# Centring part of the first row tile on ScalarE with the sign turned, all gate products of two tiles ahead of the up products, and later turns of the next tiles

## The chip, the cores and the metric

One core of one Trainium2 chip. The metric is the device time of a whole run in microseconds (us); lower is better. The time before was 921.76 us (median of 4 runs, 921.58 to 922.13).

Engines in the profile: PE is TensorE's matmuls, PEld its weight loads, DVE VectorE, ACT ScalarE, POOL GpSimd, SP SyncE. SBUF is the on-chip memory that the engines read from, PSUM the one that TensorE writes its results to, in banks. To "turn" a tile is to transpose its chunks and copy them to SBUF. "L235" is a line of the kernel. In the changed kernel the same statements have other line numbers: the transpose is L235 before and L244 after, the product L293 and L302, the copy of turned chunks L237 and L246.

## The reference, cut to what matters

```python
x  = A_x                                  # 2048 x 640, bf16
xn = layernorm(x)
s  = attention(xn @ wq, k_cache, v_cache, last 512 keys) @ wo   # 32 heads of 192
h  = sigmoid(xn @ w_gate) * (xn @ w_up)   # w_gate, w_up: 640 x 1536
g  = silu(h @ w_down)
out = x + s * g
```

The kernel computes g first, in four blocks of 512 rows, then the attention. The change touches only the first block's first 512 columns of h: the first 15 us of some 920.

## The kernel before

The first block goes by row tiles of 128 rows, t = 0 to 3. Each tile is centred (mean subtracted), its five 128x128 chunks are transposed on TensorE into PSUM, ScalarE copies the turned chunks to SBUF, and TensorE multiplies them with gate and up weights: five products of 128x512 for gate and five for up. The factor 1/std is not applied to x but later, to the products, so that the products needn't wait for it.

```python
def centred(t, parts=((0, 3 * P), (3 * P, D))):
    xc = xpool.tile([P, D], BF16, name="xn")
    for d0, d1 in parts:
        nc.vector.tensor_scalar(xc[:, d0:d1], xt[t][:, d0:d1], ln[t][:, 0:1], None,
                                op0=ALU.subtract)
    xn_t[t] = xc

def turn_pe(t, c0=0, c1=NCD, k=3):              # NCD = 5 chunks; k: PSUM bank pair
    # pT is in bank[k][:, t % 2, ...], one of the two banks of pair k (line cut)
    for c in range(c0, c1):
        nc.tensor.transpose(pT[:, c, :], xn_t[t][:, c * P:(c + 1) * P], ident[:])
    for d0, d1 in ((c0, c1),) if c1 - c0 < NCD else ((0, 3), (3, NCD)):
        nc.scalar.activation(xcT[:, d0:d1, t * P:(t + 1) * P], pT[:, d0:d1, :], AF.Copy)

def tile_half(t, fg, k, half, c0=0, c1=NCD):    # half 0: gate products, 1: up products
    ...
def tile_gated(t, fg, k):                       # sigmoid on ScalarE, product on VectorE
    ...
# start of the program (... = cuts)
centred(0, ((0, P), (P, 3 * P), (3 * P, D)))
...
turn_pe(0, 0, 1); turn_pe(0, 1, 3, 2); tile_half(0, 0, 0, 0, 0, 1)
turn_pe(0, 3, NCD, 1); tile_half(0, 0, 0, 0, 1)
turn_pe(1, 0, 3); turn_pe(1, 3, NCD, 2)
tile_half(0, 0, 0, 1, 0, 3)                     # up products of tile 0: need w_up
tile_half(1, 0, 1, 0); tile_half(0, 0, 0, 1, 3)
...
tile_gated(0, 0, 0)
for t in range(1, TQ):
    if t > 1:
        tile_half(t, 0, t % 3, 0)
    tile_half(t, 0, t % 3, 1, 0, 1)             # one up product
    if t + 1 < TQ:
        turn_pe(t + 1)                          # turn of the next tile
    tile_half(t, 0, t % 3, 1, 1)                # four up products
    tile_gated(t, 0, t % 3)
```

The softmax here doesn't subtract the row's maximum and nothing guards it: scores larger than these inputs give would overflow.

## Time and profile before

| | before |
|---|---|
| time, median (range) | 921.76 us (921.58 to 922.13) |
| span of the profiled run | 919.2 us |
| TensorE busy | 914.1 us, 99% |
| first product starts | 5.21 us |
| first up product of tile 1 | 9.29 us |
| first gate product of tile 3 | 13.13 us |

The last three rows are landmarks, read from the timeline of TensorE. X is the third product of this one, 8.86 + 2 x 0.216:

```profile
8.86 0.81 PE L293 MATMUL bank<-wu_sb,xnT 128*128 128x512 bf16 x3
```

I use the landmarks throughout. **F** is the first product, **X** the first up product of tile 1, **G** the first gate product of tile 3. The stretch F to X holds the mixed start of tiles 0 and 1. X to G holds the turns of tiles 2 and 3: 15 products and 10 transposes, 15 x 0.216 + 10 x 0.056 = 3.80 us if TensorE never waits. A timeline line gives the start, the length and a count; a product inside a merged line is found by adding 0.216 us for each product before it. Some matmul records are missing from each trace, so a count can be one short.

### The profile page before, as it was taken

To read this page: it belongs to the slowest core of one execution; us is meant where nothing else is said; L and a number is where in the kernel's file an instruction comes from. 1 tells how busy PE (TensorE), PEld (TensorE's weight loads), DVE (VectorE), ACT (ScalarE), POOL (GpSimd) and SP (SyncE) were. 2 spreads that over 40 slices of the span, in tenths; PEclk is the share of its full clock that TensorE was granted. 3 is DMA by queue.
4 is the path that set the end of the run, shared out by engine and by line. 5 is a ranking of instruction groups with operands and counts; after the bars stand their busy time and mean duration, and the time that the engine had idled before them with its cause. 6 is when DMAs were issued, how large, how long until landed. Compare 5 with 4: busy or idle time off the path is not lost.

```text
span 919.2 us, 24974 instructions
## 1 busy us (share of the span) xinstructions
PE 914.1 (99%) x11333; PEld 622.8 (68%) x11333; DVE 492.5 (54%) x989; ACT 302.3 (33%) x332; POOL 134.6 (15%) x159
## 2 busy tenths in 40 slices
PE   9999999999999999999999999999999999999998
PEld 4445455465868686867676777777776767686875
DVE  6462522444646464646555555545564646464667
ACT  4222222255141424242333333242424151515150
POOL 1000100001002000200020011001100111174733
PEclk9999999999999999999999999999999999999999
DMA  9820330115434334342425162515251615253435
GB/s 320 164 44 1 89 87 1 43 62 88 78 63 111 81 64 77 94 98 45 95 85 107 36 104 79 113 31 109 66 108 46 113 61 95 62 120 104 88 84 135
DMA packets 172106, 79.35 MB, mean 86 GB/s; under 512 B 149952, under 2 KB 167568, under 8 KB 172000
## 3 DMA queue, kind: packets, MB, share of 16 engines
q1 hardware_dynamic: 164640, 55.85, 31.1%
q0 software_dynamic: 5808, 20.52, 7.8%
q8 instruction: 88, 1.44, 0.7%
q10 hardware_dynamic: 1552, 1.39, 0.5%
q14 instruction: 18, 0.15, 0.1%
HBM read 39.45 MB, written 2.62 MB: 46 GB/s over the span
## 4 chain that ended last, share of the span: by engine, by line
PE 99%; DMA 1%; DVE 0%; SPq 0%; DVEq 0%; issue 0%
PE bank L517 22%; PE bank L446 21%; PE bank L468 19%; PE bank L428 18%; PE bank L251 8%; PE bank L263 6%; PE bank L293 3%; PE bank L394 1%; DMA wu_sb<-in_B_w_up_dram 1%; PE bank L552 0%; DVE o_sb L498 0%; DVE gate L503 0%; SPq L162 0%; PE bank L235 0%; SPq L167 0%; DVEq L654 0%
## 5 line engine op out<-in xcount | busy, mean ns | idle before, releaser
L432 ACT ACTIVATE E<-bank 128x1024 bf16<-128x1024 f32 x256 | 255.3, 1022 | 456.5 <-PE bank L428 456.4
L446 PE MATMUL bank<-xnT,wq_sb 64*128 64x512 bf16 x1800 | 226.4, 376 | 0.0
L517 PE MATMUL bank<-wo_sb,oT 64*128 64x320 bf16 x2688 | 205.2, 296 | 0.0
L428 PE MATMUL bank<-qT,kT 64*128 64x512 bf16 x1536 | 200.7, 376 | 0.0
L468 PE MATMUL bank<-vbuf,E 64*128 64x193 bf16 x4096 | 195.3, 243 | 0.0
L468 PEld LDWEIGHTS <-E 64*128 64x128 bf16 x4096 | 178.8, 94 | 10.2 <-issue 0.3
L517 PEld LDWEIGHTS <-oT 64*128 64x128 bf16 (+1 forms) x2892 | 163.2, 94 | 30.7 <-issue 0.3
L453 DVE CAST qT<-bank 128x1024 bf16<-128x1024 f32 x90 | 110.2, 1224 | 128.5 <-PE bank L446 128.5
L446 PEld LDWEIGHTS <-wq_sb 64*128 64x128 bf16 x1800 | 106.1, 100 | 87.0 <-issue 0.4
L428 PEld LDWEIGHTS <-kT 64*128 64x128 bf16 x1536 | 88.1, 94 | 73.5
L481 DVE TENSOR_TENSOR o_st<-bank,rden 128x768 bf16<-128x768 f32 x128 | 122.6, 957 | 4.4
L532 DVE TENSOR_TENSOR acc<-bank,acc 128x640 f32<-128x640 f32 x96 | 79.0, 823 | 20.2 <-PE bank L517 20.2
L118 POOL DMA_DIRECT2D vbuf<-in_A_v_cache_dram x28 | 21.1, 753 | 311.0 <-PE bank L468 308.1
L451 DVE COPY seen<-bank 128x2 f32<-128x2 f32 x90 | 14.3, 159 | 79.1 <-PE bank L446 79.1
L480 DVE RECIPROCAL rden<-bank 128x4 f32<-128x4 f32 x128 | 23.4, 182 | 60.6 <-PE bank L468 59.6
L263 PE MATMUL bank<-wd_sb,hT 128*128 128x512 bf16 (+1 forms) x384 | 52.8, 299 | 0.0
L263 PEld LDWEIGHTS <-hT 128*128 128x128 bf16 x384 | 29.7, 98 | 23.1
L251 PE MATMUL bank<-xnT,wg_sb 128*128 128x512 bf16 x180 | 44.7, 379 | 0.0
L251 PE MATMUL bank<-xnT,wu_sb 128*128 128x512 bf16 x180 | 44.7, 379 | 0.0
L257 DVE TENSOR_TENSOR hT<-bank,sig 128x512 bf16<-128x512 f32 x36 | 24.8, 690 | 37.1 <-ACT sig L254 37.1
L254 ACT ACTIVATE sig<-bank 128x512 bf16<-128x512 f32 x36 | 21.5, 597 | 55.8 <-PE bank L251 52.7
L97 POOL DMA_DIRECT2D wq_sb<-in_A_wq_dram x7 | 6.3, 900 | 210.7 <-PE bank L446 210.7
(51 smaller groups left out, 406.1 us busy)
## 6 DMA issues: line engine op xcount, KB each, us to landing
wo_sb<-in_A_wo_dram SPq DMA_DIRECT2D x7, 960.0 KB, 5.6
wq_sb<-in_A_wq_dram POOLq DMA_DIRECT2D x7, 960.0 KB, 6.1
k_st<-in_A_k_cache_dram POOLq DMA_DIRECT2D x14, 384.0 KB, 5.6
vbuf<-in_A_v_cache_dram POOLq DMA_DIRECT2D x28, 192.0 KB, 3.5
row<-in_A_x_dram POOLq DMA_DIRECT2D x16, 160.0 KB, 2.7
oT<-o_st SPq DMA_TRANSPOSE x128, 3.4
x_sb<-in_A_x_dram SPq DMA_DIRECT2D x3, 640.0 KB, 9.4
wd_sb<-in_B_w_down_dram SPq DMA_DIRECT2D x1, 1920.0 KB, 14.4
```

What stands on the lines that cost most here:

```text
L251: nc.tensor.matmul(bank[k][:, half, 0:r1 - r0], lhsT=w[:, c, f * P:(f + 1) * P], rhs=xnT[:, b, c, r0:r1], start=(c == 0), stop=(c == NCD - 1))
L257: nc.vector.tensor_tensor(hT[b][:, f, r0:r1], bank[k][:, 1, 0:r1 - r0], sig[:, 0:r1 - r0], ALU.mult)
L263: nc.tensor.matmul(wide(k)[:, d0:d1], lhsT=hT[b][:, f, q * P:(q + 1) * P], rhs=wd_sb[:, f, d0:d1], start=(f == 0), stop=(f == NF - 1))
L293: nc.tensor.matmul(bank[k][:, half, :], lhsT=xcT[:, c, t * P:(t + 1) * P], rhs=w[:, c, fg * FT:(fg + 1) * FT], start=(c == 0), stop=(c == ...
L428: nc.tensor.matmul(bank[k][:, i, :], lhsT=kT[r, pr, j, c * P:(c + 1) * P], rhs=q[r, pr * DJ + j, :], start=(j == 0), stop=(j == DJ - 1))
L432: nc.scalar.activation(E[u, pr][:, c, :, :], bank[k][:], AF.Exp, scale=scale_qk)
L446: nc.tensor.matmul(bank[k][:, half, :], lhsT=wq[r, c, col:col + DJ * (P - 1) + 1:DJ], rhs=xnT[r, b, c, :], start=(c == 0 and not second), ...
L453: nc.vector.tensor_copy(qT[u][:, 2 * m:2 * m + 2, :], bank[k][:])
L468: nc.tensor.matmul(o4[:, q, 0:DH + 1], lhsT=e[r, c, h % 2, q * P:(q + 1) * P], rhs=vbuf[r, h, c, 0:DH + 1], start=(turn == 0 and qq == 0 a ...
L481: nc.vector.tensor_tensor(o_st[u][:, :, h * DH:(h + 1) * DH], o4[:, :, 0:DH], rden[:].to_broadcast([P, TQ, DH]), ALU.mult)
L517: nc.tensor.matmul(res[:, half, :], lhsT=oT[u][r, cc, q * P:(q + 1) * P], rhs=wo[r, cc, half * HD:(half + 1) * HD], start=(turn == 0 and c ...
L532: nc.vector.tensor_tensor(cols(acc[:, t, :]), res, cols(acc[:, t, :]), ALU.add)
```

## The change

The intent, as far as the diff shows it: take 256-wide pieces of the centring off VectorE at the very start, so that tile 1 is centred sooner; fill the wait for the up weights with the gate products of tile 1; and put the turns of tile 1 among the gate products of tile 0. ScalarE computes bias + scale * x, so with the mean as bias it gives mean - x. The sign is turned everywhere, and the factor is negated on GpSimd. The up products before each turn become three instead of one.

```diff
 def stats_root(t):
+    if t < TQ:
+        minus[t] = bwork.tile([P, 1], F32, name="minus")
+        nc.gpsimd.tensor_scalar(minus[t][:], rstd[:], -1.0, None, op0=ALU.mult)
...
-def centred(t, parts=((0, 3 * P), (3 * P, D))):
+def centred(t, parts=((0, 3 * P), (3 * P, D)), on_act=0):
     ...
+    for i, (d0, d1) in enumerate(parts):
+        if i < len(parts) - on_act:
+            nc.vector.tensor_scalar(xc[:, d0:d1], xt[t][:, d0:d1], ln[t][:, 0:1], -1.0,
+                                    op0=ALU.subtract, op1=ALU.mult)
+        else:
+            nc.scalar.activation(xc[:, d0:d1], xt[t][:, d0:d1], AF.Identity,
+                                 bias=ln[t][:, 0:1], scale=-1.0)
...
 def tile_gated(t, fg, k, between=None):
-    rstd = ln[t][1]
+    rstd = minus[t]
...
-centred(0, ((0, P), (P, 3 * P), (3 * P, D)))
+centred(0, ((0, P), (P, 3 * P), (3 * P, D)), 2)
...
-tile_half(0, 0, 0, 0, 1)
+tile_half(0, 0, 0, 0, 1, 3)
 turn_pe(1, 0, 3)
+tile_half(0, 0, 0, 0, 3)
 turn_pe(1, 3, NCD, 2)
-tile_half(0, 0, 0, 1, 0, 3)
 tile_half(1, 0, 1, 0)
-tile_half(0, 0, 0, 1, 3)
+tile_half(0, 0, 0, 1)
...
-tile_gated(0, 0, 0)
 for t in range(1, TQ):
     ...
-    tile_half(t, 0, t % 3, 1, 0, 1)
+    tile_half(t, 0, t % 3, 1, 0, 3)
     if t + 1 < TQ:
         turn_pe(t + 1)
-    tile_half(t, 0, t % 3, 1, 1)
+    tile_half(t, 0, t % 3, 1, 3)
+    if t == 1:
+        tile_gated(0, 0, 0)
     tile_gated(t, 0, t % 3)
```

More of the change, by code (lines that the diff above doesn't have):

```diff
@@ L222 @@
         xn_t = {}
-        def centred(t, parts=((0, 3 * P), (3 * P, D))):
+        minus = {}
+        def centred(t, parts=((0, 3 * P), (3 * P, D)), on_act=0):
             xc = xpool.tile([P, D], BF16, name="xn")
-            for d0, d1 in parts:
-                nc.vector.tensor_scalar(xc[:, d0:d1], xt[t][:, d0:d1], ln[t][:, 0:1], None,
-                                        op0=ALU.subtract)
+            for i, (d0, d1) in enumerate(parts):
[5 more added lines that the diff above has]
+                                         bias=ln[t][:, 0:1], scale=-1.0)
             xn_t[t] = xc
```

## The prediction

> **What bounds the kernel now.** I read the page first: busy shares, then the chain that ended last, then the idle time in the groups.
>
> ```profile
> PE 914.1 (99%) x11333; PEld 622.8 (68%) x11333; DVE 492.5 (54%) x989; ACT 302.3 (33%) x332; POOL 134.6 (15%) x159
> ...
> PE 99%; DMA 1%; DVE 0%; SPq 0%; DVEq 0%; issue 0%
> ...
> L446 PE MATMUL bank<-xnT,wq_sb 64*128 64x512 bf16 x1800 | 226.4, 376 | 0.0
> L517 PE MATMUL bank<-wo_sb,oT 64*128 64x320 bf16 x2688 | 205.2, 296 | 0.0
> ```
>
> TensorE works 914.1 of 919.2 us, the chain is TensorE for 99%, and the big matmul groups have no idle time before them. So the change, which keeps every product and every transpose and only changes their order and what feeds them, can win or lose only bubbles of the TensorE stream, all in the first 13 us. The waits of the weight loads (PEld) up to 16 us show how much there is:
>
> ```profile
> PEld L293 <- ACT xnT L237: 1.4, 4, 0.5
> PEld L194 <- DVE warm L169: 1.1, 1, 1.1
> PEld L235 <- DVE xn L227: 0.3, 1, 0.3
> PEld L293 <- issue: 0.2, 1, 0.2
> ```
>
> Then the timeline of TensorE from 4 us, to place them (columns: start us, length us, engine, line, operation, names, shapes; L235 is a transpose, L293 a product):
>
> ```profile
> 4.54 0.48 PE L235 MATMUL bank<-ident,xn 128*128 128x128 bf16 x3
> 5.21 0.38 PE L293 MATMUL bank<-wg_sb,xnT 128*128 128x512 bf16 x1 [0.19 <-DMA wg_sb<-in_B_w_gate_dram]
> 5.43 0.27 PE L235 MATMUL bank<-ident,xn 128*128 128x128 bf16 x2
> 5.54 1.24 PE L293 MATMUL bank<-wg_sb,xnT 128*128 128x512 bf16 x4
> 6.62 0.44 PE L235 MATMUL bank<-ident,xn 128*128 128x128 bf16 x5
> 7.14 0.81 PE L293 MATMUL bank<-wu_sb,xnT 128*128 128x512 bf16 x3
> 7.78 1.24 PE L293 MATMUL bank<-wg_sb,xnT 128*128 128x512 bf16 x5
> ```
>
> A 512-wide product follows another every 0.216 us (later five take 1.08), a transpose every 0.056 us; the printed lengths contain overlapping drain. From the first transpose (4.54) to the gate product of row tile 3 (13.13, below) there are 20 transposes and 30 products: 20 x 0.056 + 30 x 0.216 = 7.60 us of work in 8.59 us. So the bubbles there sum to about 1.0 us: 0.14 and 0.35 before the first product, 0.21 within the first tile's gate products (four products and the one step to the next transpose take 6.62 - 5.54 = 1.08, of which 0.87 is work), 0.24 before the first up product (7.14; its weights landed at 7.10), and 0.03 at the turn of tile 2. This 1.0 us, 0.11% of the time, is all that the change could win. From 7.14 on the chain names nothing but TensorE.
>
> **What the Trainium skill says.** "TensorE: Matmul & The Clock Gate", section "Back-to-back issue gap", gives N/2.4 + 2.5 ns for a warm product, 216 ns at 512: the trace agrees (0.216). The same page, section "Step-by-step: what each phase is for", says that weight loads are pulled ahead but matmuls stay in program order, so a product that waits holds up all behind it; the trace shows no product out of program order. "ScalarE: Activation LUTs", section "What ACT_TABLE_LOAD costs", gives 186 ns + 0.833 N ns with immediates and about 93 ns more for each pointer operand, and back-to-back overlap of about 93 ns. In the trace, the 512-wide sigmoid with a pointer scale takes 687 ns and that without 597, a difference of 90, and the two copies of one turn overlap by about 0.10. The same page, section "Table sets: the hidden batching unit", says that copy and identity are in every set; the trace has Copy after Sigmoid with a single table load, and Identity isn't shown yet.
>
> **Part 1, centring on ScalarE.** Of three VectorE pieces of tile 0 (254, 281 and 282 ns, beginning 4.23, last end 4.88) the two 256-wide ones go to ScalarE. Each: 186 + 93 + 213 = 492 ns, an estimate from that page's figures (the trace's 256-wide copy from PSUM with immediates is 383). The means are ready at 4.20, so ScalarE runs 4.25 to 4.75 and 4.65 to 5.15. VectorE had ended these chunks at 4.68 and 4.88: 0.07 and 0.27 later, not earlier. ScalarE is in order and the copy of the first turned chunk (4.81 before) comes behind both in the program: about 5.05 to 5.33, so the first product goes from 5.21 to 5.38. In exchange VectorE starts on tile 1 0.39 us earlier: its first centred piece ends at 5.88 in place of 6.27. Turning the sign with a second immediate operation I count as free.
>
> **Part 2, new order of the first two tiles.** I ran the list forward with the latencies of the trace: VectorE to weight load 0.05, last transpose's end to copy 0.04, copy to weight load 0.05. Gate products of tile 0: c0 5.38; transposes 3 and 4 5.60; c1, c2 5.71; three transposes of tile 1 6.14 (their data is ready at 5.93, so the earlier VectorE is used); c3 6.35, c4 6.57; the other transposes 6.79. Free at 6.90. Now the gate products of tile 1 need the copy of the three chunks: last transposed at 6.47, copied 6.51 to 6.99, first product 7.05: a bubble of 0.15 replaces the wait for the up weights. Ten products, then the first up product of tile 1 at 7.05 + 10 x 0.216 = 9.21, where before it was at 9.29. **Gain 0.09 us**, most of it uncertain.
>
> **Part 3, the turns of tiles 2 and 3.** The turn of the next tile now comes after three up products, leaving two between the turn and the next gate product, where there were four. Before, at tile 3:
>
> ```profile
> 11.99 0.44 PE L235 MATMUL bank<-ident,xn 128*128 128x128 bf16 x5
> ...
> 12.27 1.03 PE L293 MATMUL bank<-wu_sb,xnT 128*128 128x512 bf16 x4
> 12.47 0.77 ACT L237 ACTIVATE xnT<-bank 128x384 bf16<-128x384 bf16 x2 [0.87 <-PE bank L235]
> 13.01 17.06 PEld L293 LDWEIGHTS <-xnT 128*128 128x128 bf16 x80 [0.21 <-ACT xnT L237]
> 13.13 1.24 PE L293 MATMUL bank<-wg_sb,xnT 128*128 128x512 bf16 x5
> ```
>
> Read it as a race. ScalarE's copy starts when all five transposes have ended (12.43, not the third); it takes 0.49, and the next weight load is released at 13.01: 1.02 us after the first transpose. TensorE meanwhile has 0.28 of transposes and 4 x 0.216 = 0.86 of products, 1.14 us: the copy is hidden with 0.12 to spare. With two products TensorE has 0.28 + 0.43 = 0.71 us and must wait 1.02 - 0.71 = **0.31 us, at tile 2 and again at tile 3**: 0.62. Saved: the 0.03 at tile 2, which came from a sigmoid ahead of the copy, as the sigmoid of tile 0 now stands behind it. The deferred sigmoid and product of tile 0 hold bank 0 until about 2.6 and 3.3 us after that 9.21; tile 3 wants it 4.4 us after, so no wait from there.
>
> **Part 4, the negated factor on GpSimd.** Four operations on 128x1. The power operations take 548 ns, so the negations take at most about that. The first factors are ready by about 8 us, the first sigmoid now runs after 10.5. Off the path.
>
> **Sum.** -0.09 + 0.62 - 0.03 = +0.5 us. Nothing absorbs a shift afterwards as TensorE streams to the end: 921.93 + 0.5 = 922.4.
>
> **Rivals.** (a) **The intent holds**: earlier VectorE and the gate-first order take away the 0.21 and 0.24 bubbles and the turns cost nothing: -0.4 us, 921.5. For it: both bubbles exist, and the wait for weights does go. Against it: the copy's 0.80 from the last transpose to the product is longer than two products. It would need the copy to start at the third transpose, and then 0.20 would still be left each time: about +0.25 in total. (b) **Table loads**: if Identity needed another set, a load of 1.28 us (the trace's one load) before the centring and one back before the sigmoid; the first is on the path and costs over 1.2 us, the second stands mostly beside products: 923.5 to 924.5. The page speaks against it. (c) **ScalarE is the bound at the start**: if its SBUF-source pieces take 0.6 each, everything in part 2 is 0.1 to 0.2 later and the gain is gone: 922.5 to 922.7. (d) **No visible change**: 0.5 us is as wide as the spread of the three runs (921.6 to 922.13), so the medians may hardly differ.
>
> **Range and chances.** Half of the 0.5 us is run spread, and (a) to (c) lie from 921.5 to 924. I give 921.6 to 923.0 eight in ten. Over 2% is 18 us; no rival comes near: same 0.98.
>
> **What would show it.** Right: in the timeline of the changed kernel, two new idle times of about 0.3 us of the weight loads behind the copies L237 near 10.5 to 11 and 13 to 13.5 us; pieces of about 0.49 us on ScalarE from 4.25; first product near 5.4; first up product of tile 1 near 9.2; one table load. Wrong: no idle weight load at those turns (rival a), a second table load (b), pieces far from 0.49 (c), or a TensorE bubble after 14 us that the kernel before lacks.

## The result, and the profile after

The changed kernel took **922.54 us** (median of 4 runs, 921.88 to 923.38) against 921.76. The ratio is 1.0008, with a 95% interval from 0.9991 to 1.0026. A ratio here is the mean time of one kernel's runs over that of the other's in the same rounds, so it is not quite the ratio of the medians quoted. The interval includes no change at all: what follows rests on the traces more than on the times.

The timeline of TensorE in the changed kernel (start us, length us, engine, line, operation, names, shapes, count, idle before):

```profile
5.74 0.38 PE L302 MATMUL bank<-wg_sb,xnT 128*128 128x512 bf16 x1 [0.69 <-DMA wg_sb<-in_B_w_gate_dram]
...
8.50 1.89 PE L302 MATMUL bank<-wu_sb,xnT 128*128 128x512 bf16 x8
10.23 0.44 PE L244 MATMUL bank<-ident,xn 128*128 128x128 bf16 x5
10.72 0.38 PE L302 MATMUL bank<-wu_sb,xnT 128*128 128x512 bf16 x1
11.25 1.25 PE L302 MATMUL bank<-wg_sb,xnT 128*128 128x512 bf16 x5 [0.15 <-ACT xnT L246]
...
12.99 0.44 PE L244 MATMUL bank<-ident,xn 128*128 128x128 bf16 x5
13.27 0.59 PE L302 MATMUL bank<-wu_sb,xnT 128*128 128x512 bf16 x2
14.01 1.25 PE L302 MATMUL bank<-wg_sb,xnT 128*128 128x512 bf16 x5
```

The reader is to see the starts, not the printed idle times, which the modelled drain of a product shortens. After the turn at 12.99 come two up products, 13.27 and 13.48; the next could start at 13.70, and starts at 14.01. That is 0.31 us of nothing, and the same again before 11.25 (the last up product started at 10.72; 10.94 would have been possible). X is at 8.50 + 5 x 0.216 = 9.58, so X to G is 14.01 - 9.58 = 4.43 us where it was 3.84.

The waits of the weight loads up to 16 us, one line, to hold against the first line of the same view before (columns: total us, times, longest):

```profile
PEld L302 <- ACT xnT L246: 2.0, 5, 0.6
```

The wait for ScalarE's copies went from 1.4 to 2.0 us. What ScalarE did, from its timeline:

```profile
1.65 1.28 ACT L187 ACT_TABLE_LOAD   x1 [1.65 <-DVE wg_sb L172]
...
4.21 0.91 ACT L236 ACTIVATE xn<-x_sb,mv 128x256 bf16<-128x256 bf16 x2 [1.06 <-DVE mv L206]
...
10.71 0.77 ACT L246 ACTIVATE xnT<-bank 128x384 bf16<-128x384 bf16 x2 [2.86 <-PE bank L244]
```

The two centring pieces take 0.91 us together from 4.21, and there is still one table load. The copy at 10.71 stands right behind the end of the fifth transpose; ScalarE had been idle for 2.86 us before it, so it isn't ScalarE's load that makes the product late.

And the negation, from the groups of GpSimd in the first 16 us (count | busy us, mean ns | idle before):

```profile
L216 POOL TENSOR_SCALAR minus<-rstd 128x1 f32<-128x1 f32 x4 | 0.9, 224 | 0.4
```

**Where the span went.** The spans are 919.2 and 920.7 us, 1.5 apart; the profiled runs' times are 921.03 and 922.45. By landmarks: F is 0.53 later (5.74 - 5.21), as the first gate weights landed at 5.70; F to X is 0.24 shorter (3.84 for 4.08); X to G is 0.59 longer; and from G to the end the changed kernel took 906.7 and the kernel before 906.1. 0.53 - 0.24 + 0.59 + 0.6 = 1.5. Only two of these four terms were in the prediction as such. The experiments had to tell which of them belong to the change.

### The profile page after: what moved, and what is told of

Same layout as the page of the kernel before. It is cut to its first block, busy times and chain, and to the rows that moved or that the text cites. A ratio compares the mean times of both kernels' runs of the same rounds, so it can differ in the third digit from the quotient of the medians.

```text
span 920.7 us, 24960 instructions
## 1 busy us (share of the span) xinstructions
PE 913.5 (99%) x11314; PEld 623.1 (68%) x11333; DVE 494.3 (54%) x987; ACT 302.9 (33%) x334; POOL 134.9 (15%) x163
## 3 DMA queue, kind: packets, MB, share of 16 engines
q10 hardware_dynamic: 1552, 1.39, 0.5%
## 4 chain that ended last, share of the span: by engine, by line
PE 98%; DVE 1%; DMA 0%; issue 0%; ACT 0%; DVEq 0%
PE bank L527 22%; PE bank L456 21%; PE bank L478 19%; PE bank L438 18%; PE bank L260 8%; PE bank L272 6%; PE bank L302 3%; PE bank L404 1%; DMA wg_sb<-in_B_w_gate_dram 0%; PE bank L562 0%; DVE gate L513 0%; DVE o_sb L508 0%; ACT xnT L246 0%; PE bank L244 0%; DVEq L664 0%
## 5 line engine op out<-in xcount | busy, mean ns | idle before, releaser
L527 PE MATMUL bank<-wo_sb,oT 64*128 64x320 bf16 x2688 | 205.2, 296 | 0.0
L478 PE MATMUL bank<-vbuf,E 64*128 64x193 bf16 x4096 | 195.3, 243 | 0.3 <-DVE o_sb L508 0.3
L478 PEld LDWEIGHTS <-E 64*128 64x128 bf16 x4096 | 178.8, 94 | 10.7 <-issue 1.1
L527 PEld LDWEIGHTS <-oT 64*128 64x128 bf16 (+1 forms) x2892 | 163.4, 94 | 30.6 <-issue 0.3
L272 PE MATMUL bank<-wd_sb,hT 128*128 128x128 bf16 (+1 forms) x377 | 52.4, 298 | 0.4
```

Source lines behind the costliest of these rows:

```text
L272: nc.tensor.matmul(wide(k)[:, d0:d1], lhsT=hT[b][:, f, q * P:(q + 1) * P], rhs=wd_sb[:, f, d0:d1], start=(f == 0), stop=(f == NF - 1))
L478: nc.tensor.matmul(o4[:, q, 0:DH + 1], lhsT=e[r, c, h % 2, q * P:(q + 1) * P], rhs=vbuf[r, h, c, 0:DH + 1], start=(turn == 0 and qq == 0 a ...
L527: nc.tensor.matmul(res[:, half, :], lhsT=oT[u][r, cc, q * P:(q + 1) * P], rhs=wo[r, cc, half * HD:(half + 1) * HD], start=(turn == 0 and c ...
```

## The experiments

Twelve runs were made, of nine new kernels and of three kernels once more, all with correct results. This is the list of landmarks from all profiles, in us, with the medians of the timed runs beside those of the kernel before in the same rounds:

| run | F | X | G | F to X | X to G | median | before |
|---|---|---|---|---|---|---|---|
| kernel before | 5.21 | 9.29 | 13.13 | 4.08 | 3.84 | 921.76 | |
| e12, before again | 5.39 | 9.73 | 13.57 | 4.34 | 3.84 | 921.47 | 921.81 |
| changed kernel | 5.74 | 9.58 | 14.01 | 3.84 | 4.43 | 922.54 | 921.76 |
| e10, changed again | 5.46 | 9.31 | 13.75 | 3.85 | 4.44 | 922.26 | 921.71 |
| e1, turn after 1 | 5.33 | 9.18 | 12.98 | 3.85 | 3.80 | 921.29 | 921.63 |
| e11, turn after 1 again | 5.34 | 9.78 | 13.58 | 4.44 | 3.80 | 921.45 | 921.71 |
| e2, before, turn after 3 | 6.22 | 10.06 | 14.50 | 3.84 | 4.44 | 922.15 | 921.63 |
| e3, turn after 5 | 5.62 | 9.86 | 15.16 | 4.24 | 5.30 | 922.85 | 921.63 |
| e9, copies of 2 and 3 | 5.39 | 9.25 | 13.47 | 3.86 | 4.22 | 921.70 | 921.71 |
| e5, turn in two calls | 5.44 | 9.29 | 14.61 | 3.85 | 5.32 | 923.16 | 921.53 |
| e4, no ScalarE centring | 5.33 | 9.49 | 13.92 | 4.16 | 4.43 | 922.30 | 921.63 |
| e6, before, ScalarE centring | 5.45 | 9.63 | 13.46 | 4.18 | 3.83 | 922.03 | 921.53 |
| e7, before, order alone | 5.34 | 9.62 | 13.45 | 4.28 | 3.83 | 921.66 | 921.53 |
| e8, first weights in two | 5.43 | 9.45 | 13.24 | 4.02 | 3.79 | 922.15 | 921.53 |

The column X to G is what repeats: it differs by at most 0.01 us between profiles of kernels that have the same turns and the first sigmoid at the same place (ahead of the first copy in the kernel before, e6 and e7, 3.83 to 3.84; behind it in e1, e11 and e8, 3.79 to 3.80). F and F to X move from run to run with the same program (e1 against e11, before against e12).

### Are the later turns the loss? (e1, e2)

```diff
 # e1: the changed kernel with
-            tile_half(t, 0, t % 3, 1, 0, 3)
+            tile_half(t, 0, t % 3, 1, 0, 1)
             if t + 1 < TQ:
                 turn_pe(t + 1)
-            tile_half(t, 0, t % 3, 1, 3)
+            tile_half(t, 0, t % 3, 1, 1)
 # e2: the kernel before with the opposite edit
```

Expected of e1:

> The changed kernel with one thing put back: the turns of tiles 2 and 3 come after one up product again (four products between turn and gate product). Theory (two products are too short to hide the copy): the two idle times of about 0.31 us on TensorE behind the turns of tiles 2 and 3 vanish, from the first up product of tile 1 to the first gate product of tile 3 takes 3.80 us in place of 4.43, and the time falls by 0.6 us against the changed kernel, to 0.1 us of the kernel before. Rival (the loss comes from the centring on ScalarE or from the start's loads): that stretch stays within 0.1 us of 4.43 or the time stays at +0.5 us or more over before.

Expected of e2:

> The kernel before with only the turns of tiles 2 and 3 moved behind three up products. Theory: the stretch from the first up product of tile 1 to the first gate product of tile 3 grows from 3.84 to about 4.43 us (twice 0.31 of idle, less the 0.03 wait behind the sigmoid), and the time grows by 0.6 us. Rival (it takes the change's other parts to lose): the stretch and the time stay within 0.1 us of before.

The timeline of TensorE in e1:

```profile
8.10 1.46 PE L302 MATMUL bank<-wu_sb,xnT 128*128 128x512 bf16 x6
9.40 0.44 PE L244 MATMUL bank<-ident,xn 128*128 128x128 bf16 x5
9.68 1.03 PE L302 MATMUL bank<-wu_sb,xnT 128*128 128x512 bf16 x4
10.54 1.24 PE L302 MATMUL bank<-wg_sb,xnT 128*128 128x512 bf16 x5
...
12.98 1.24 PE L302 MATMUL bank<-wg_sb,xnT 128*128 128x512 bf16 x5
```

Turn at 9.40, four products from 9.68, gate product at 10.54: 9.68 + 4 x 0.216, no gap. X to G is 3.80, the floor. In e2 it is 4.44, as in the changed kernel, with none of the change's other parts: turns at 10.71 and 13.48, and the gate products behind them at 11.74 and 14.50, 1.03 and 1.02 us later. So the later turns alone add 0.6 us to this stretch, in either kernel, and taking them back removes it. The rivals of both runs are out as far as the stretch goes. In time, e1 measured 921.29 against 921.63 and e2 922.15 against 921.63: in the expected directions, both with intervals that include 1 (0.9982 to 1.0007; 0.9992 to 1.0017), so the times alone settle neither.

### Does the idle follow the race of copy against products? (e3, e9)

```diff
 # e3: the changed kernel with the turn after all five
-            tile_half(t, 0, t % 3, 1, 0, 3)
+            tile_half(t, 0, t % 3, 1)
             if t + 1 < TQ:
                 turn_pe(t + 1)
-            tile_half(t, 0, t % 3, 1, 3)
 # e9: the changed kernel with the first copy of two chunks
-            for d0, d1 in ((c0, c1),) if c1 - c0 < NCD else ((0, 3), (3, NCD)):
+            for d0, d1 in ((c0, c1),) if c1 - c0 < NCD else ((0, 2), (2, NCD)):
```

Expected of e3:

> The changed kernel with the turns after all five up products, none left to hide the copy. Theory (race of 1.02 us against 0.28 plus 0.216 for each product): idle of 0.74 us at each of two turns, the stretch from the first up product of tile 1 to the first gate product of tile 3 takes 5.29 us, the time rises by 0.86 us over the changed kernel. Rival (an idle time of fixed length from the semaphores or from PSUM): the idle stays near 0.31 each, and the time that of the changed kernel.

Expected of e9:

> The changed kernel with the copies of the turns of tiles 2 and 3 cut as two and three chunks in place of three and two; the program of TensorE is untouched. Theory (the idle behind a turn is the wait for the first copy): that copy takes 0.38 in place of 0.49 us, so the idle falls from 0.31 to 0.21 at each turn and the stretch from the first up product of tile 1 to the first gate product of tile 3 from 4.43 to 4.22 us; the second copy is still in time for the third product. Rival (the product waits for both copies, or for the transposes alone): the stretch stays at 4.43 or grows.

TensorE in e3, then in e9:

```profile
10.94 0.44 PE L244 MATMUL bank<-ident,xn 128*128 128x128 bf16 x5
11.96 1.25 PE L302 MATMUL bank<-wg_sb,xnT 128*128 128x512 bf16 x5 [0.58 <-ACT xnT L246]
```

```profile
9.89 0.44 PE L244 MATMUL bank<-ident,xn 128*128 128x128 bf16 x5
10.17 0.59 PE L302 MATMUL bank<-wu_sb,xnT 128*128 128x512 bf16 x2
10.81 1.25 PE L302 MATMUL bank<-wg_sb,xnT 128*128 128x512 bf16 x5
```

In e3 the gate product follows the turn by 11.96 - 10.94 = 1.02 us, the length of the race that the prediction read off the kernel before, with only 0.28 us of transposes beside it. X to G is 5.30 for an expected 5.29, and the time is 922.85 against 921.63 (ratio 1.0013, 1.0001 to 1.0026: the interval excludes no change). The expected rise of 0.86 us over the changed kernel isn't to be seen in the times: the medians, from different rounds, are 0.31 apart. In e9 the product follows by 0.92 in place of 1.02, just what a first copy of 0.38 in place of 0.49 us gives, and X to G is 4.22 as expected. Dose and response agree for zero, two and four products behind the turn and for two lengths of the copy. Its time, 921.70 against 921.71, is lower than the changed kernel's 922.26 of the same rounds, though the ranges overlap (921.56 to 922.89 and 921.84 to 922.79).

### What does the first copy wait for? (e5)

```diff
             if t + 1 < TQ:
-                turn_pe(t + 1)
+                turn_pe(t + 1, 0, 3)
+                turn_pe(t + 1, 3, NCD)
```

> The changed kernel with the turns of tiles 2 and 3 still after three up products, but each turned and copied in two calls (three chunks and their copy, then two chunks and their copy), which lets the first copy wait for the third transpose only. Theory (the copy waits for the last transpose that was put into the program ahead of it on the same bank, then 0.80 us to the product): the copy starts 0.11 us earlier, the idle time falls from 0.31 to about 0.20 us at each turn, the stretch from the first up product of tile 1 to the first gate product of tile 3 takes about 4.20 us in place of 4.43. Rival (the wait is for something else, such as the bank's earlier readers): the stretch stays at 4.43.

A miss: X to G is 5.32, not 4.20, and the time is 923.16 against 921.53, the slowest of all. TensorE in e5:

```profile
9.98 0.33 PE L244 MATMUL bank<-ident,xn 128*128 128x128 bf16 x3
10.89 0.27 PE L244 MATMUL bank<-ident,xn 128*128 128x128 bf16 x2 [0.58 <-ACT xnT L246]
```

The first half of the expectation held: the copy started at 10.35 in ScalarE's timeline, 0.37 us after the first transpose, where it had been 0.48 (10.23 to 10.71 in the changed kernel). The second half failed: the other two transposes waited until that copy had ended, 0.74 us after they could have started (9.98 + 3 x 0.056 = 10.15). They write other columns of the same bank that the copy reads. The Trainium skill, "PSUM — Partial Sum Buffer", section "PSUM bank collisions raise a hardware error", says that accesses of two engines to one bank (and the same group of 32 partitions in it) have to be kept apart by semaphores whatever their addresses. The traces agree with a program that waits by bank: a copy waits for the last transpose put ahead of it on its bank, and a later transpose waits for the copy. The other three bank pairs are in use at that point (tile 0's results not yet taken, tile 1's being summed, tile 2's next). But the turn uses only one bank of its own pair, `t % 2`; whether the last two chunks could go to the other one, so that they don't wait, was not tried.

### What are the new start's parts worth? (e4, e6, e7)

```diff
 # e4: the changed kernel, all of tile 0 centred on VectorE
-        centred(0, ((0, P), (P, 3 * P), (3 * P, D)), 2)
+        centred(0, ((0, P), (P, 3 * P), (3 * P, D)))
 # e6: the kernel before with minus and centred() of the changed kernel, order as before
-        centred(0, ((0, P), (P, 3 * P), (3 * P, D)))
+        centred(0, ((0, P), (P, 3 * P), (3 * P, D)), 2)
-            rstd = ln[t][1]
+            rstd = minus[t]
 # e7: the kernel before, order of tiles 0 and 1 alone; turns of tiles 2, 3 after one product
-        tile_half(0, 0, 0, 0, 1)
+        tile_half(0, 0, 0, 0, 1, 3)
         turn_pe(1, 0, 3)
+        tile_half(0, 0, 0, 0, 3)
         turn_pe(1, 3, NCD, 2)
-        tile_half(0, 0, 0, 1, 0, 3)
         tile_half(1, 0, 1, 0)
-        tile_half(0, 0, 0, 1, 3)
+        tile_half(0, 0, 0, 1)
```

Expected of e4:

> The changed kernel with all three pieces of tile 0 centred on VectorE, sign still turned. Theory: the first product is then bound by the arrival of its weights; tile 1's centring ends some 0.4 us later, its transposes wait for it, and from the first product to the first up product of tile 1 takes up to 4.2 us in place of 3.84 when the weights come early, so the time is 0 to 0.2 us above the changed kernel. Rival (ScalarE's queue at the start is what costs the 0.5 us): the time falls by 0.2 us or more.

Expected of e6:

> The kernel before with the centring of two pieces of tile 0 on ScalarE and the turned sign alone. Theory: in the old order the earlier VectorE helps nobody, as the transposes of tile 1 come after all gate products of tile 0; from the first product to the first up product of tile 1 takes 3.84 to 4.08 us as the up weights land late or early against it, from there to the first gate product of tile 3 3.80 to 3.84; the time stays within 0.3 us of before. Rival (the centring on ScalarE gains or costs by itself): one of the stretches leaves these limits, or the time moves by 0.5 us or more.

Expected of e7:

> The kernel before with the gate products of both tiles first and the split turn of tile 1 among those of tile 0, all centring on VectorE, turns of tiles 2 and 3 after one product. Theory: with early weights the transposes of tile 1 wait for VectorE, and the stretch from the first product to the first up product of tile 1 is about 4.15 us, as in the changed kernel without ScalarE centring (4.16), no better than the 4.08 of before; the second stretch is 3.80 to 3.86; the time within 0.3 us of before. Rival (the order alone is the gain): 3.84 us or less in the first stretch with a first product before 5.4 us.

e4 against e1, which have the same F of 5.33: without ScalarE's share the transposes of tile 1 waited for VectorE, started at 6.39 in place of 6.10, and F to X grew from 3.85 to 4.16 us. So with early weights the ScalarE centring was worth 0.31 us in the new order, by one profile of each. One part of the expectation missed: the copy of the first chunk (from 5.00 us), and not the weights, released the first product of e4. Its time, 922.30, is 0.24 below the changed kernel's 922.54, as the rival asked, but from other rounds, and 0.04 above that of e10: not resolved. e6 put the same centring into the old order: X to G as expected at 3.83, F to X 4.18, a little outside of the limits named (3.84 to 4.08), which by the letter is the rival's sign; 922.03 against 921.53, not resolved. e7, the order alone: F to X 4.28 for an expected 4.15, 921.66 against 921.53.

The two misses of 0.1 us have a visible cause: in e6 and e7 (and e3 and e11) the first products ran at a slower pace. In e11 the transpose behind the first product started 0.40 us after it, in e1 0.22. The Trainium skill, "TensorE: Matmul & The Clock Gate", section "What's actually happening", says that the array starts at half its clock and that the moment of the full pace differs between runs of one kernel; by the formula for the slow pace in its section "Back-to-back issue gap", N/1.2 ns, 512 columns would take 427 ns (an estimate). The traces agree, with 0.40. In e7 the slow pace also hid what was to be tested: VectorE had the first three chunks of tile 1 centred at 6.31 us, and TensorE came to their transposes only at 6.53. So e7 doesn't tell whether the order alone gains anything. The pace makes F to X comparable only between profiles that were at full pace by then: before, e12, changed, e1, e2, e4, e5, e8, e9 and e10.

### The kernels once more (e10, e11, e12)

No edits: the changed kernel and e1 side by side in one set of rounds, and a second profile of the kernel before.

> The changed kernel itself once more, beside the version with the turns after one product, to compare them on one chip. Theory: stretch from the first up product of tile 1 to the first gate product of tile 3 again 4.43 us; the first product starts when its weights land, somewhere from 5.3 to 6.2 us, otherwise than in its first profile; the time 0.3 to 0.8 us over the kernel before.

> The changed kernel with the turns after one product, once more in the same rounds. Theory: 0.6 us (0.4 to 0.9) below the changed kernel and within 0.4 us of the kernel before, the stretch 3.80 us. Rival: what the first comparison showed was luck of the loads, and the two agree within 0.2 us.

> The kernel before itself, for a second profile of its start. Theory (the start differs from run to run by the arrival of the first loads and by when TensorE reaches its full pace): the first product lies somewhere from 5.2 to 6.2 us, the stretch from it to the first up product of tile 1 anywhere from 3.84 to 4.3 us, and from there to the first gate product of tile 3 3.80 to 3.84 us as before. Rival (the start of the kernel before is always as in its first profile): 5.21 and 4.08 us again within 0.05.

On one chip the changed kernel took 922.26 us (921.84 to 922.79) and the version with turns after one product 921.45 (920.94 to 921.51): the ranges of five runs each don't overlap, 0.81 us between the medians. The turns account for 0.64 (4.44 - 3.80). But that the two numbers are close is chance: the spans of the two profiles also differ by 0.8, and by landmarks e11 against e10 has -0.12 in F, +0.59 in F to X (the slow pace), -0.64 in X to G and -0.6 from G to the end. e10's first product was not set by its weights, which landed at about 5.2 (issued at 1.17, 4.0 us to landing), but by ScalarE's copy: F was 5.46. That part of its expectation missed.

e12 refutes its rival (5.39 and 4.34 for 5.21 and 4.08; 4.34 is 0.04 above the range expected) and shows what the start of the kernel before hangs on. First the chain of work in the first profile of the kernel before, then in e12, then in e1 (start us, length us, what):

```profile
2.13 4.96 DMA wu_sb<-in_B_w_up_dram
7.10 0.04 issue
7.14 2.53 PE bank L293 x11
```

```profile
2.14 5.40 DMA wu_sb<-in_B_w_up_dram
7.53 0.04 issue
7.58 2.53 PE bank L293 x11
```

```profile
4.19 0.91 ACT xn L236 x2
5.09 0.19 ACT xnT L246
5.28 0.05 issue
5.33 0.39 PE bank L302
```

In both profiles of the kernel before, X is the landing of the up weights plus 2.2 us, and that landing moved from 7.10 to 7.53: X moved from 9.29 to 9.73. In e1 the chain runs through ScalarE's centring and the up weights are not in it. In the changed kernel's own first profile it was the load of the first gate weights.

### An attempt to beat both (e8)

```diff
-        load_f(nc.scalar, wg_sb, wg_r, 0, 4, 0, 3)
+        load_f(nc.scalar, wg_sb, wg_r, 0, 4, 0, 1)
+        load_f(nc.scalar, wg_sb, wg_r, 0, 4, 1, 3)
```

This is e1 with the first load of gate weights cut in two.

> Meant to beat both: the changed kernel with the turns after one product, and the first load of gate weights (three chunks, 384 KB, that landed between 5.0 and 6.2 us in the runs so far) cut in two, chunk 0 first. Theory (the start is set by the arrival of these weights in most runs, and that differs from run to run by over 1 us): chunk 0 lands before 5.0, the first product starts at 5.3 behind the copy on ScalarE, chunks 1 and 2 arrive no later than now; the time is 921.0 to 921.3, some 0.3 to 0.5 us below the kernel before of the same rounds, with less spread. Rival (bandwidth: the loads behind are delayed by as much, or chunk 1 becomes the wait): the first product or the second waits as now and the time is that of the turns after one product alone.

It failed by its rival: chunk 0 landed early, 2.7 us after its issue, and F was 5.43, behind the copy. But chunks 1 and 2 landed only at about 5.9, and the second product started at 5.94 where 5.77 would have followed the transposes. The time was 922.15 against 921.53, with a spread from 921.71 to 925.08, more and not less (ratio 1.0013, 1.0000 to 1.0026). That is more than the turns after one product took; why, was not looked into.

So the best version is e1. Its ten runs in two sets of rounds lie from 920.94 to 921.51, and those of the kernel before from 921.16 to 922.61. Both intervals of the ratio (0.9982 to 1.0007 and 0.9982 to 1.0009) include 1, so that it beats the kernel before is likely but not settled; that it beats the changed kernel by some 0.8 us is seen in the same rounds.

## Why the prediction was right or wrong

The time was right: 922.54 us measured, 922.4 predicted, range 921.6 to 923.0. That the median came so close is in part luck, as the steps show; the difference from the kernel before is itself not resolved by the times.

**What bounds the kernel** was right: TensorE is 99% busy in all profiles and what the change moved lies before 14 us, with one exception told below. But bubbles don't lie in the first 13 us alone: from 860 to 919 us TensorE was busy for 55.45 of 59 us in the kernel before.

**Part 1** was right in its mechanism and sizes. The pieces took 507 and 492 ns for an estimate of 492, from 4.21; the second one ended at 5.12 for 5.15. Turning the sign cost VectorE nothing: three pieces take 0.65 us in e4 as before. VectorE began on tile 1 at 4.36 in e1 and 4.51 in e10, where it was 4.79 before; in the first profile of the changed kernel it waited for the rows of tile 1 until 4.91. The first product behind ScalarE's copy was put at 5.38; where the weights came early it was at 5.33 to 5.46 (e1, e5, e9, e10). The first profile of the changed kernel had 5.74, as its weights landed at 5.70, which the prediction did not reckon with.

**Part 2** had the stretch right, and the gain ill-founded. F to X was put at 9.21 - 5.38 = 3.83 and measured 3.84 and 3.85. But "Gain 0.09 us" set a forecast against the one X of one profile, 9.29, and that X hangs on a load whose landing moved by 0.43 us between two profiles of the same kernel. The new order takes this load off the chain; what that is worth depends on the loads. X lay at 9.29 and 9.73 before and at 9.58 and 9.31 in the changed kernel, so that a pair of profiles shows anything from 0.29 lost to 0.42 gained. And the old order has 3.84 as well when its first product comes late enough that the up weights are there: e2, with F at 6.22. The mechanism stands; the size of the gain is not shown.

**Part 3** was right. Idle of 0.31 us twice was predicted; X to G grew by 0.59 and 0.60 us for the 0.62 less 0.03 predicted. e1 and e2 show that it is the turns, e3 and e9 that it is the race.

**Part 4** was right, with room: the negation takes 224 ns for at most 548.

**The sum** left a term out. "Nothing absorbs a shift afterwards as TensorE streams to the end" looks only for gaps that would close, and the last sentence named "a TensorE bubble after 14 us that the kernel before lacks" as a sign of being wrong. There is one. GpSimd, VectorE and TensorE in the changed kernel, late:

```profile
880.02 1.39 POOL L547 TENSOR_TENSOR acc<-acc,row 128x640 f32<-128x640 f32 x1 [0.75 <-DMA row<-in_A_x_dram]
880.13 1.96 DVE L513 TENSOR_TENSOR gate<-o_sb,acc 128x640 bf16<-128x640 f32 x1
...
882.02 0.81 DVE L508 TENSOR_TENSOR o_sb<-bank,gate 128x640 f32<-128x640 f32 x1
...
882.88 0.84 PE L478 MATMUL bank<-vbuf,E 64*128 64x193 bf16 x16 [0.29 <-DVE o_sb L508]
```

The first VectorE operation (L513) takes 0.82 us when nothing is beside it. Here it took 1.96, with a GpSimd operation on the same kind of tile from 880.02 to 881.41; the next VectorE operation freed a bank 1.1 us late, and TensorE went on at 882.88 where its rhythm (0.65 us after 881.76) would have had it at 882.41. The Trainium skill, "SBUF — State Buffer", section "SBUF: two separate sides", says that VectorE and GpSimd share a port pair, that a VectorE operation with two SBUF inputs and a GpSimd operation that reads SBUF exclude each other, and that the one which starts second fully blocks. The traces agree: the longer one ended 0.68 us after GpSimd's (at 881.41 + 0.68), as in e10 and in the kernel before (0.69 each), where a whole one takes 0.82; and in e2, where the VectorE operation began first (880.62, GpSimd 880.63), it kept its 0.82 us and GpSimd took 2.07 in place of 1.39.

From G to the end the changed kernel took 906.7 us in both its profiles, and the kernel before 906.1 in both of its own (919.7 - 13.57 = 906.1 for e12). The whole difference arises here: from G to the last group of L527 products ahead of this place (L517 before) it is 865.62 us in both profiles of the changed kernel and 865.61 and 865.60 in those of the kernel before; the next stretch, up to the fifth group of L478 products (L468), takes 7.25 and 7.30 against 6.72 in both of the kernel before. So of the 1.5 us between the first two profiles 0.5 to 0.6 is this collision.

Is it of the change's making? The other profiles speak against a simple link. e2 and e4 have the same late turns and show no such stop of TensorE (906.1 and 906.4 from G to the end); e8 has its turns after one product and shows it (906.7). The rest lie between 906.1 (e11) and 906.5. GpSimd's start there is released by the landing of a row of x, so where TensorE stands against the loads can decide who collides; whether the changed kernel makes it more frequent, or two profiles out of two were chance, stays open. The prediction's 0.5 us came out near the measured 0.8 with this term not counted at all, with a start whose gain or loss changes from run to run, and with times that scatter by 0.5 us and more.

**Rivals.** (a), the turns cost nothing, is refuted by X to G; its remark that a copy released by the third transpose would still leave 0.20 each was not testable, as e5 shows, because the bank is held. (b), table loads: one load, refuted. (c), ScalarE slower at 0.6 us a piece: refuted by 507 and 492 ns. (d), no visible change in the times: true of every single comparison of the changed kernel with the kernel before.

## What to carry to other kernels

When work is moved behind other work on a full engine, count what is left in front of the consumer: here two products (0.43 us) could not hide a turn, a copy and a release (1.02 us with the transposes' own 0.28), and four could. A gain measured against one profile of a start that waits for loads is worth no more than the spread of those landings, so take two profiles of the kernel before ahead of such a change. And within a few tenths of a microsecond, compare stretches between landmarks in the trace that depend on no load and begin after TensorE has its full pace: X to G repeated to 0.01 us where the times of one kernel scatter by 0.5 us and more, and F to X did not (3.85 and 4.44 in e1 and e11).

## What the Trainium skill lacked or had wrong

- "PSUM — Partial Sum Buffer", "PSUM bank collisions raise a hardware error": it gives the rule by bank and quadrant, and not what it costs a pipeline. Here a copy of chunks 0 to 2 that waits for transposes 3 and 4 of the same bank starts 0.11 us later (0.48 against 0.37 us after the first transpose), and two transposes that wait for a copy on their bank lost 0.74 us.
- "TensorE: Matmul & The Clock Gate", section "What you observe": the step to full pace is put about 4 us into sustained work, give or take 0.5 (the next section calls it run-variable). The spread was wider here. TensorE started at about 1.05 us in these kernels. In the first profile of the kernel before, the last two of its 256-wide warm-up products started 0.10 us apart (4.16 and 4.26), where they had been 0.21 apart until 4.02; in e11 a 512-wide product at 5.96 us still took 0.42. So the step came from at most 3.2 (4.26 - 1.05) to at least 5.3 us (6.38 - 1.05) after the start, though in e11 with short waits of TensorE on the way.
- "TensorE: Matmul & The Clock Gate", section "Back-to-back issue gap", which the prediction cites: it calls the 216 ns the gap of an isolated product and names about 131 ns for 512 columns in a stream with weight loads. In the streams of these runs, a weight load for each product, it is 0.216 us: five 128x512 products take 1.08.
- No page has the spread of a load's time at the start of a kernel: the same 384 KB of gate weights took 3.9 us from issue to landing in e1, 4.5 in the changed kernel and 5.0 in e2.
- No page has the time of a tiny GpSimd operation: 224 ns for a multiply of 128x1 and 544 to 568 for a power.
